# Attention and GEGLU on one core: value products ahead of the second exponential tile in all steps with a counted ScalarE backlog

## The chip, the core and the metric

The kernel runs on one core of a Trainium2 chip. The core has five engines, each with its own stream of instructions, that meet only through semaphores: TensorE (PE, matrix products; PEld are its weight loads), VectorE (DVE), ScalarE (ACT), GpSimd (POOL) and SyncE (SP, which issues the transfers). Matrix products land in PSUM, which has eight banks here of 128 x 512 float32. The metric is the device time of one execution in microseconds (us), lower is better. The kernel before took 1220.43 us, the median of three runs between 1219.77 and 1221.08.

## The reference

A transformer block on x of 2048 x 512 in bfloat16, with 32 heads of 16 columns, followed by a gated feed-forward layer of width 1792:

```
h   = x + attention(layernorm(x))           # q,k,v = x @ wqkv ; o @ wo
        scores = (q @ k^T) * 16**-0.5        # 32 heads, 2048 x 2048 each
        p = softmax(scores) ; o = p @ v
h2  = h + (gelu(n @ w_gate) * (n @ w_up)) @ w_down,   n = layernorm(h)
```

With 32 heads the scores are 32 x 2048 x 2048 numbers, and each of them passes VectorE once (for the maximum of its row) and ScalarE once (for its exponential).

## The kernel before, in words

**A program that is written by a planner.** The Python code is run once when the kernel is built. It walks through a loop of *ticks* (variable `tick`, L1645 to L1755), and in each tick it appends instructions to the lists of the five engines. A class `Plan` records for each buffer who wrote and who read it last and puts in the semaphore waits. An engine runs its own list strictly in this order. What stands behind a waiting instruction on the same engine waits as well. `group_begin` and `group_end` collect all waits of the instructions between them at the first one.

**Units.** The attention is cut into 64 units (`units`). A unit is 16 ticks long and covers four heads and 256 rows of queries (in the last units eight heads and 128 rows) against all 2048 keys. It is passed through twice. In the first pass (p1) a *score pair* of two 128 x 512 tiles is computed per tick (`p1_pair`, matmul at L886, into PSUM banks 0 to 3, two pairs of banks in turn) and VectorE takes the row maxima of both tiles in one instruction (`p1_consume`, L901). GpSimd turns the maxima of a unit into a correction of the queries (`negm_part`, `negm_pre`, `negm_post`). In the second pass (p2), 24 ticks behind the first (`P2_START`), the transposed scores are computed again, now with the maximum subtracted, in two *tiles* per tick (`p2_tile`, matmuls at L977). ScalarE takes the exponential of each (`p2_consume`, L1006) and writes it to a ring of tiles (PTM, PTE, PTG). These tiles use PSUM banks 4 to 7.

**Joint units.** In 14 units (`JOINT`) the tick with remainder 14 is dropped: its row maxima and those of the tick with remainder 10 are taken together at the latter by a fused add and maximum (L898), which uses differences of scores made ahead of time by `item_diff` (L1110, L1112) and taken out of PSUM by ScalarE (L1115). The dropped tick puts the second pass behind (`behind`), and it catches up with a third tile in some odd ticks (`more`).

**Dense items.** All other matrix work is cut into items of a few *pieces*: projections (`item_projT`, `item_projV`), value products (`item_pv`), output projection (`item_oproj`), gate, up and down (`item_gate`, `item_up`, `item_down` and their halves), differences. `dense.piece()` emits one piece and returns its cost in columns. One piece is emitted per tick, as a rule after both exponential tiles of that tick. Where no piece is at hand, `dummy` (L1621) puts in filling matmuls, whose results nobody uses.

**Value products.** `item_pv(ui)` multiplies the exponentials of a unit with the values. It has four pieces, `p` = 0 to 3, due at the ticks with remainders 7, 8, 9 and 10, each of 16 or 32 small matmuls (L1023). After the last one ScalarE copies the sum out of PSUM to `OB` (through `evac_act`, L730), and a transfer (L1051) and GpSimd (L1065, L1070) do the rest.

**PSUM banks of the second pass.** Banks 4 to 7 stand in one list, `banks.free`; `take` removes the first, `give` appends at the end. A tile takes a bank when its matmuls are emitted and gives it back when its exponential is emitted. A dense item keeps a bank from its first to its last piece. A later taker's matmul waits on the semaphore of the ScalarE instruction that read the bank last.

**The order in a tick.** The score pair and the first tile (one group of waits), the second tile, in some ticks a third one, then the row maxima, the exponentials, then the dense piece or fill:

```
            t2l = [next_tile()] if p2_ok and p1_ok else []
            P.group_end("pe")
            if p2_ok and p1_ok:
                behind[0] -= 1
                if dense.plain and tick - th_step[0] == 2 and not more:
                    mid = dense.piece()
                t2l.append(next_tile())
```

So there is an exception (L1692): two ticks after a tanh of the feed-forward part was put on ScalarE (`th_step`, set at L1297), and if the next piece is one of the middle pieces of a value product (`dense.plain`, set at L1028 to be true ahead of pieces 1 and 2, false ahead of the last), that piece is emitted ahead of the second tile.

**The count of ScalarE's backlog.** `act_lag` is the planner's estimate, in us, of the work that ScalarE has been given beyond what it can do: `act_tick` adds 0.478 for each exponential of the tick and takes off 1.135 for the tick, `act_more` adds the cost of other work. It is a number in the program and not measured.

Of the kernel before, what the change touches and what calls it, by code (L numbers as in the profile page):

```python
# [248 lines left out]
def bass_sequential_preLN__mha_block__geglu_ffn__prompt_kernel(nc, A_x, A_wqkv, A_wo, B_x, B_w_gate, B_w_up, B_w_down, out):  # L249
    dbg = None  # L250
    with ExitStack() as es:
# [81 lines left out]
        OB = at("OB", [128, 2, 256], BF16)  # L333
# [10 lines left out]
        pbank = es.enter_context(nc.psum_tensor("pbank", [128, 8, 512], FP32))  # L344
# [195 lines left out]
        class Dense:  # L540
            def __init__(self):
                self.prio = []
                self.ready = []
                self.extra = []
                self.gen = None
                self.under = None
                self.plain = False
                self.bank = None
                self.banks = [7, 3, 4, 5]
                self.rr = 0  # L550
                self.pause = 0
                self.single = False
                self.done = 0
                self.now = 0
# [152 lines left out]
        pool = PoolStream()  # L707

        act_lag = [0.0]
        th_step = [-9]  # L710
        def act_more(cost):
            act_lag[0] += cost
        def act_tick(exps):
            act_lag[0] = max(0.0, act_lag[0] + 0.478 * exps - 1.135)
        dve_free = [False]

        def evac_act(o_ap, i_ap, reads, writes, scale=None, extra=(), bias=None, then=None, cost=0.48):
# [291 lines left out]
        def item_pv(b, ui, ps=(0, 1, 2, 3)):  # L1009

            gi, slot = units[ui]
            pt_t = PV_T if ui < NU - 1 else PV_TL
            for p in ps:
                while not force[0] and dense.now < P2_START + 16 * ui + pt_t[p]:
                    yield ("wait", 1)
                for m in (2 * p, 2 * p + 1):
                    n, c0, s_ = (2, 0, slot) if ui < UB else (4, 128 * (m // 4), slot + m // 4)
                    qn = 512 // n
                    for i in range(n):
                        kt = 2 * m + i if ui < UB else 4 * (m % 4) + i  # L1020
                        for g in range(4):
                            pi = pt_of[(ui, m, g)]
                            P.op("pe", lambda e, g=g, kt=kt, pi=pi, i=i, s_=s_, c0=c0, qn=qn: e.matmul(pbank[32 * g:32 * g + 17, b, c0:c0 + qn], VA[:, kt, 4 * s_ + g, :],  # L1023
                                                                                                      PTt(pi)[:, qn * i:qn * i + qn], start=(kt == 0), stop=(kt == NT - 1), tile_position=(0, 32 * g)),
                                 reads=[("V", kt), "VA_ones", ("PT", pi)], writes=[("pb", b)], sig=(g == 3 and i == n - 1))
                    for g in range(4):
                        pt_busy.discard(pt_of.pop((ui, m, g)))
                dense.plain = p != ps[-1] and p + 1 != ps[-1]  # L1028
                if p != ps[-1]:
                    yield 2  # L1030
            if ui == NU - 1:
                col = ps[0] // 2
                evac_act(OA[:, 1, 256 * col:256 * col + 128], pbank[:, b, 128 * col:128 * col + 128], [("pb", b)], [("OA", 1, col), ("RB", 1)], cost=0.2)
                if col == 0:
                    dense.add(item_ofin, gi, front=True, est=3, not_before=dense.now + 3)
                    return 2
            else:
                evac_act(OB[:, ui % 2, :], pbank[:, b, 0:256], [("pb", b)], [("OB", ui % 2)], cost=0.27, then=lambda: o_turn(ui))
            pv_done.add(ui)
            return 2  # L1040

# [4 lines left out]
        def o_turn(ui):  # L1046
            gi, slot = units[ui]
            par = ui % 2
            assert not ob_busy.get(par), "GpSimd too far behind"
            ob_busy[par] = True  # L1050
            P.dma("sp", lambda e: e.dma_start_transpose(out=OBT[:, par, :, :], in_=OB[:, par, :]), ("obT", par), reads=[("OB", par)], writes=[("OBT", par)])  # L1051
            o4 = OBT[:, par].rearrange("p q (g i) -> p q g i", i=32)
            ks, slots = ((0, 1), (slot,)) if ui < UB else ((half(ui),), (slot, slot + 1))
            defer(5, lambda: o_norm(gi, slots, ks, par, o4, ("OBT", par), ob_busy))
# [229 lines left out]
        def gelu_chain(par, dE, w=512):  # L1284

            th_ready[par] = False
            gs, ts_ = g_sb[:, par, 0:w], th_sb[:, par, 0:w]
            o = lambda cost, fn, reads, extra=(): (cost if w == 512 else 0.6 * cost, lambda: P.op("pool", fn, reads=reads, writes=[("th", par)], extra_deps=extra))
            def later(n):
                if not force[0] and (tight() or dense.gen is not None and dense.cur is item_pv and dense.now % 16 in (9, 10)):  # L1290
                    defer(1, lambda: later(n))
                    return
                if not force[0] and (act_lag[0] + (0.48 if dense.gen is not None and dense.cur in (item_gate, item_up, item_gate_h, item_up_h) else 0) > LAG_TH + SLOPE * n or poly_end[par] > TICK * dense.now + POLY):
                    defer(1, lambda: later(n + 1))
                    return
                act_more(0.54 if w == 512 else 0.32)
                th_step[0] = dense.now  # L1297
                P.op("act", lambda e: e.activation(out=ts_, in_=ts_, func=ACT.Tanh, scale=GC), reads=[("th", par)], writes=[("th", par)])  # L1298
                defer(1, second)
            def poly_done():  # L1300
                poly_end[par] = pool.t
                defer(TANH_LAG, lambda: later(0))
            def second():
                def done():
                    th_ready[par] = True
                pool.add([o(0.62, lambda e: e.tensor_scalar(out=ts_, in0=ts_, scalar1=1.0, scalar2=0.5, op0=ALU.add, op1=ALU.mult), [("th", par)]),  # L1306
                          o(1.27, lambda e: e.tensor_tensor(out=ts_, in0=ts_, in1=gs, op=ALU.mult), [("th", par), ("g", par)])], then=done)  # L1307
            pool.add([o(1.04, lambda e: e.tensor_tensor(out=ts_, in0=gs, in1=gs, op=ALU.mult), [("g", par)], dE),  # L1308
                      o(0.62, lambda e: e.tensor_scalar(out=ts_, in0=ts_, scalar1=0.044715, scalar2=1.0, op0=ALU.mult, op1=ALU.add), [("th", par)]),
                      o(1.27, lambda e: e.tensor_tensor(out=ts_, in0=ts_, in1=gs, op=ALU.mult), [("th", par), ("g", par)])], then=poly_done)  # L1310
# [325 lines left out]
        J_ = sorted(JOINT)  # L1636
        J_PREP = {max(60, 16 * (J_[i - 1] if i else 0) + 12, 16 * J_[i] - 48 if J_[i] > 50 else 0): J_[i] for i in range(len(J_))}
        ticking[0] = True
        def next_tile():
            n = 2 * t2 - behind[0]  # L1640
            st, jj = n // 2, n % 2
            ui_ = st // 16
            t = p2_tile(ui_, st % 16, 1 - (st + P2_START) % 2, jj)
            return ui_, t
        while True:  # L1645
            p1_ok = tick < 16 * NU
# [42 lines left out]
            P.group_end("pe")  # L1689
            if p2_ok and p1_ok:  # L1690
                behind[0] -= 1
                if dense.plain and tick - th_step[0] == 2 and not more:  # L1692
                    mid = dense.piece()
                t2l.append(next_tile())
                if more:
                    behind[0] -= 1
                    t2l.append(next_tile())
                behind[0] += 1
            elif p2_ok and tick % 2 == 0:
                if tick == 16 * NU:  # L1700
                    dense.ready.sort(key=lambda it: it[0] is item_down)
                    own = dense.bank if dense.gen is not None else banks.free[0]
                    other = own ^ 1
                    banks.free = [other] if dense.gen is not None else [own, other]
                    pairs = [0, 2, 10 - (own & 6)]
                for d_ in ((0, 1) if t2 + 1 < 16 * NU else (0,)):
                    b_ = pairs.pop(0)
                    pairs.append(b_)
                    ui_, j_ = (t2 + d_) // 16, (t2 + d_) % 16
                    p2_pair(ui_, [p2_tile(ui_, j_, 1 - (tick + d_) % 2, jj, b_ + jj) for jj in (0, 1)])  # L1710
# [7 lines left out]
                    unit_end(tick // 16)  # L1718
            for ui_, t in t2l:
                p2_consume(ui_, [t])  # L1720
            if p2_ok and t2 % 16 == 0:
                if t2 // 16 < NU - 1:
                    dense.add(item_pv, t2 // 16, front=True, est=5, not_before=tick + PV_T[0])
                else:
                    for p_ in (0, 2):
                        dense.add(item_pv, NU - 1, (p_, p_ + 1), front=True, est=2, not_before=tick + PV_TL[p_])
# [71 lines left out]
```

## Time and profile before

| | |
|---|---|
| median of the runs | 1220.43 us (1219.77 to 1221.08) |
| the profiled execution | 1219.59 us, of which its span from first to last instruction is 1217.5 us |
| granted TensorE clock | 1.000 |
| row maxima L901, VectorE | 996 instructions, 1134.2 us busy, 5.7 us idle ahead of them |
| exponentials L1006, ScalarE | 2000 instructions (1357 into PTM, 407 into PTG, 236 into PTE), 1105.0 us busy, 5.1 us idle ahead of them |
| tanh L1298, ScalarE | 50 instructions, 42.9 us busy |
| copies to OB L730, ScalarE | 62 instructions, 28.3 us busy, 390 to 693 ns each |
| score pairs L886, TensorE | 2020 matmuls, 388.5 us busy |
| tiles L977, TensorE | 5120 matmuls, 513.6 us busy |
| value products L1023, TensorE | 126.0, 51.2 and 41.8 us busy by source |
| fill L1621, TensorE | 659 matmuls, 208.3 us busy |

Busy times are unions: instructions of one engine overlap in part, so a mean duration times a count is more than the busy time. The idle time of a group is that of its engine just ahead of its instructions. The profile is of one execution; its steady part, with both passes running, lies between about 45 and 1173 us from the start, and the remainder after the last row maxima is some 44 us.

### The profile page before, as it was taken

The page shows a single profiled execution, that of the slowest core. Times are in us where ns is not written, and L with a number is a line of the kernel's source. Part 1 is how long each engine was busy: PE and PEld are TensorE (multiplying, and loading weights), DVE is VectorE, ACT ScalarE, POOL GpSimd, SP SyncE. Part 2 cuts the span into 40 slices and gives each one's busy share as a digit, 9 for nine tenths or more (in the row PEclk, how much of TensorE's full clock was granted, in tenths as well). Part 3 has the DMA queues.
Part 4 walks back from the last instruction along what each step waited for, and adds up shares of the span by engine and source line. Part 5 has one row for each costly group of instructions (what it writes and reads, how often), then busy time and mean ns, then how long its engine had stood idle before and what let it go on. Part 6 is the DMA issues. An engine that isn't in the chain of part 4 may idle for free.

```text
span 1217.5 us, 35931 instructions
## 1 busy us (share of the span) xinstructions
PE 1103.6 (91%) x14692; PEld 476.7 (39%) x14838; DVE 1180.5 (97%) x1125; ACT 1188.8 (98%) x2422; POOL 837.9 (69%) x1772
## 2 busy tenths in 40 slices
PE   7899888889999989999899989999899989998998
PEld 3233332233333333334333333333334454554666
DVE  8999999999999999999999999999999999999973
ACT  7899999999999999999999999999999999999995
POOL 8567684756777586766868487684777687846772
DMA  5111104300010000110001000100001100010000
GB/s 154 28 34 27 29 24 136 93 8 11 8 28 21 12 9 10 25 23 12 10 22 17 23 8 10 25 21 15 8 8 29 26 18 16 9 27 15 18 16 19
DMA packets 69651, 32.02 MB, mean 26 GB/s; under 512 B 54768, under 2 KB 68464, under 8 KB 69488
## 3 DMA queue, kind: packets, MB, share of 16 engines
q1 hardware_dynamic: 69488, 29.71, 9.9%
q8 instruction: 118, 1.93, 0.6%
q14 instruction: 45, 0.37, 0.1%
HBM read 11.80 MB, written 2.10 MB: 11 GB/s over the span
## 4 chain that ended last, share of the span: by engine, by line
ACT 50%; DVE 40%; PE 8%; issue 2%; DMA 1%; POOL 1%
DVE PM L901 38%; ACT PTM L1006 28%; ACT PTG L1006 9%; ACT PTE L1006 5%; PE pbank L1427 2%; ACT g_sb L730 2%; ACT u_sb L730 2%; ACT th_sb L1298 1%; PE pbank L977 1%; PE pbank L1328 1%; PE pbank L886 1%; ACT OB L730 1%; DVE OA L898 1%; ACT OA L1115 1%; PE pbank L1621 1%
## 5 line engine op out<-in xcount | busy, mean ns | idle before, releaser
L901 DVE TENSOR_REDUCE PM<-pbank 128x2 f32<-128x1024 f32 x996 | 1134.2, 1215 | 5.7 <-PE pbank L977 1.8
L1006 ACT ACTIVATE PTM<-pbank 128x512 bf16<-128x512 f32 x1357 | 736.3, 737 | 3.5 <-PE pbank L977 0.6
L977 PE MATMUL pbank<-QT,KT 32*128 32x256 bf16 (+1 forms) x5120 | 513.6, 250 | 8.4 <-ACT PTG L1006 0.4
L886 PE MATMUL pbank<-KT,QT 32*128 32x512 bf16 x2020 | 388.5, 384 | 23.9 <-DVE PM L901 8.6
L1621 PE MATMUL pbank<-ones_bf,ident 128*128 128x512 bf16 x659 | 208.3, 384 | 51.8 <-ACT PTM L1006 21.7
L977 PEld LDWEIGHTS pbank<-QT,KT 32*128 32x128 bf16 x5120 | 207.6, 92 | 70.4 <-ACT PTM L1006 37.7
L886 PEld LDWEIGHTS pbank<-KT,QT 32*128 32x128 bf16 x2020 | 96.6, 91 | 341.9 <-DVE PM L901 126.7
L1006 ACT ACTIVATE PTG<-pbank 128x512 bf16<-128x512 f32 x407 | 227.0, 728 | 0.8 <-PE pbank L977 0.4
L1006 ACT ACTIVATE PTE<-pbank 128x512 bf16<-128x512 f32 x236 | 141.7, 735 | 0.8 <-PE pbank L977 0.5
L1023 PE MATMUL pbank<-PTM,VA 128*17 128x256 bf16 (+1 forms) x3470 | 126.0, 252 | 2.0 <-ACT PTM L994 0.4
L1065 POOL TENSOR_TENSOR LINV<-OBT,negone 128x8 f32<-128x8 bf16 x63 | 105.0, 1667 | 5.8 <-DMA OBT<-OB 5.6
L1621 PEld LDWEIGHTS pbank<-ones_bf,ident 128*128 128x128 bf16 x767 | 44.6, 97 | 134.1 <-ACT PTM L1006 85.3
L1308 POOL TENSOR_TENSOR th_sb<-g_sb 128x512 f32<-128x512 f32 (+1 forms) x50 | 51.1, 1022 | 63.0 <-ACT g_sb L730 63.0
L1023 PEld LDWEIGHTS pbank<-PTM,VA 128*17 128x17 bf16 x3470 | 67.0, 90 | 40.9 <-issue 21.7
L956 POOL TENSOR_TENSOR QT<-QT,STG 128x256 bf16<-128x256 bf16 x64 | 42.7, 667 | 33.9 <-DMA STG<-ST 33.4
L1307 POOL TENSOR_TENSOR th_sb<-th_sb,g_sb 128x512 f32<-128x512 f32 (+1 forms) x50 | 62.2, 1245 | 4.0
L1310 POOL TENSOR_TENSOR th_sb<-th_sb,g_sb 128x512 f32<-128x512 f32 (+1 forms) x50 | 62.3, 1246 | 1.7
L1306 POOL TENSOR_SCALAR th_sb<-th_sb 128x512 f32<-128x512 f32 (+1 forms) x50 | 30.5, 609 | 44.9 <-ACT th_sb L1298 44.8
L1427 PE MATMUL pbank<-wd_sb,GUT 128*128 128x512 bf16 x191 | 54.5, 382 | 3.4 <-ACT PTM L1006 0.8
L801 POOL TENSOR_SCALAR QT<-QKS,qmask 128x512 bf16<-128x512 bf16 x30 | 46.9, 1566 | 13.6 <-ACT QKS L730 12.8
L1383 PE MATMUL pbank<-hnT_l,wg_sb 128*128 128x256 bf16 x336 | 51.2, 275 | 3.3 <-ACT PTM L1006 0.7
L1419 POOL TENSOR_TENSOR GUT<-th_sb,u_sb 128x512 bf16<-128x512 f32 x42 | 53.3, 1268 | 1.3
(197 smaller groups left out, 1208.8 us busy)
## 6 DMA issues: line engine op xcount, KB each, us to landing
QKS<-QKS SPq DMA_DIRECT2D x27, 112.0 KB, 2.1
x_sb<-in_A_x_dram SPq DMA_DIRECT2D x4, 512.0 KB, 5.7
xres<-in_A_x_dram SPq DMA_DIRECT2D x16, 128.0 KB, 2.3
out_dram<-out_sb SPq DMA_DIRECT2D x15, 128.0 KB, 1.7
wg_sb<-in_B_w_gate_dram SPq DMA_DIRECT2D x4, 448.0 KB, 4.2
wu_sb<-in_B_w_up_dram SPq DMA_DIRECT2D x4, 448.0 KB, 4.0
wd_sb<-in_B_w_down_dram SPq DMA_DIRECT2D x3, 512.0 KB, 4.5
STG<-ST SPq DMA_TRANSPOSE x64, 2.3
```

The costliest lines, as they stand in the source:

```text
L730: P.op("act", lambda e: e.activation(out=o_ap, in_=i_ap, func=ACT.Copy, **kw), reads=reads, writes=writes, extra_deps=extra)
L886: P.op("pe", lambda e, g=g, b=b: e.matmul(pbank[:, b, :], QT[32 * g:32 * g + 32, c, slot, 128 * qt:128 * qt + 128], KT[32 * g:32 * g + 32, ...
L901: P.op("dve", lambda e: e.tensor_reduce(out=PM[:, par, qt, kc, g:g + 2], in_=pbank[:, b:b + 2, :], axis=AX.X, op=ALU.max), reads=[("pb", b ...
L977: P.op("pe", lambda e, kt=kt, i=i: e.matmul(pbank[:, b, qn * i:qn * i + qn], KT[32 * g:32 * g + 32, slot, 128 * kt:128 * kt + 128], QT[32 ...
L1006: P.op("act", lambda e, b=b, pi=pi: e.activation(out=PTt(pi), in_=pbank[:, b, :], func=ACT.Exp), reads=[("pb", b)], writes=[("PT", pi)], e ...
L1023: P.op("pe", lambda e, g=g, kt=kt, pi=pi, i=i, s_=s_, c0=c0, qn=qn: e.matmul(pbank[32 * g:32 * g + 17, b, c0:c0 + qn], VA[:, kt, 4 * s_ + ...
L1065: P.op("pool", lambda e: e.tensor_tensor(out=li, in0=o4[:, :, :, 16], in1=negone[:, 0:4 * nq].rearrange("p (q h) -> p q h", q=nq), op=ALU. ...
L1307: o(1.27, lambda e: e.tensor_tensor(out=ts_, in0=ts_, in1=gs, op=ALU.mult), [("th", par), ("g", par)])], then=done)
L1310: o(1.27, lambda e: e.tensor_tensor(out=ts_, in0=ts_, in1=gs, op=ALU.mult), [("th", par), ("g", par)])], then=poly_done)
L1419: P.op("pool", lambda e: e.tensor_tensor(out=o_ap, in0=shp(ts_), in1=shp(us), op=ALU.mult), reads=[("th", par), ("u", par)], writes=o_keys ...
L1427: P.op("pe", lambda e: e.matmul(pbank[:, b, :], GUT[:, fc, 128 * k:128 * k + 128], wd_sb[:, fc, :], start=first, stop=last), reads=[("GUT" ...
L1621: P.op("pe", lambda e: e.matmul(pbank[:, b, :], ident[:], ones_bf[:, 0:512], start=True, stop=True), reads=["ident", "ones_bf"], writes=[( ...
```

## The change

The condition for the exception is changed, and the last piece of a value product is admitted to it. Five parts:

- `th_step` goes. In its place `lag_was` keeps the count of the backlog as it stood at the last two ticks, and the piece is moved ahead of the second tile where the older of the two is at least 0.2 us (`LAG_MID`), whatever ScalarE work it came from.
- `dense.plain` is now true ahead of the last piece as well.
- The bank of the second tile is taken ahead of the piece, and handed to `next_tile` and `p2_tile`.
- While the moved piece is emitted, `dense.midway` is set. A last piece then does not emit ScalarE's copy to OB at once but puts it in `dense.held`, and it is emitted after the tick's exponentials. So ScalarE's order stays.
- The item itself ends inside the moved piece, and with it its bank is given back there, ahead of the tick's two tiles.

```
+        lag_was = [0.0, 0.0]
+        LAG_MID = 0.2
...
             act_lag[0] = max(0.0, act_lag[0] + 0.478 * exps - 1.135)
+            lag_was[:] = [lag_was[1], act_lag[0]]
...
-                dense.plain = p != ps[-1] and p + 1 != ps[-1]
+                dense.plain = p != ps[-1]
...
-                evac_act(OB[:, ui % 2, :], pbank[:, b, 0:256], [("pb", b)], [("OB", ui % 2)], cost=0.27, then=lambda: o_turn(ui))
+                def out():
+                    evac_act(OB[:, ui % 2, :], pbank[:, b, 0:256], [("pb", b)], [("OB", ui % 2)], cost=0.27, then=lambda: o_turn(ui))
+                    pv_done.add(ui)
+                if dense.midway:
+                    dense.held.append(out)
+                    return 2
+                out()
             pv_done.add(ui)
             return 2
...
-                th_step[0] = dense.now
...
-        def next_tile():
+        def next_tile(bank=None):
             n = 2 * t2 - behind[0]
             st, jj = n // 2, n % 2
             ui_ = st // 16
-            t = p2_tile(ui_, st % 16, 1 - (st + P2_START) % 2, jj)
+            t = p2_tile(ui_, st % 16, 1 - (st + P2_START) % 2, jj, bank)
...
                 behind[0] -= 1
-                if dense.plain and tick - th_step[0] == 2 and not more:
+                b_ = banks.take()
+                if dense.plain and lag_was[0] >= LAG_MID and not more:
+                    dense.midway = True
                     mid = dense.piece()
-                t2l.append(next_tile())
+                    dense.midway = False
+                t2l.append(next_tile(b_))
...
             for ui_, t in t2l:
                 p2_consume(ui_, [t])
+            while dense.held:
+                dense.held.pop(0)()
```

## The prediction, as it was put on record

> **What bounds the kernel now.** I read the page's busy times first, then its chain of waits, then the timeline of single ticks (a tick is one pass of the main loop: one score pair for VectorE, two exponential tiles for ScalarE, one dense piece).
>
> ```profile
> PE 1103.6 (91%) x14692; PEld 476.7 (39%) x14838; DVE 1180.5 (97%) x1125; ACT 1188.8 (98%) x2422; POOL 837.9 (69%) x1772
> ...
> ACT 50%; DVE 40%; PE 8%; issue 2%; DMA 1%; POOL 1%
> ...
> L901 DVE TENSOR_REDUCE PM<-pbank 128x2 f32<-128x1024 f32 x996 | 1134.2, 1215 | 5.7 <-PE pbank L977 1.8
> ```
>
> VectorE and ScalarE are both nearly full, and the chain changes between them. VectorE has the firmer limit: 996 maximum reductions (L901) with 5.7 us of idle time in all. Where nothing is late they follow each other at 1.13 us:
>
> ```profile
> 640.68 5.74 DVE L901 TENSOR_REDUCE PM<-pbank 128x2 f32<-128x1024 f32 x5
> ```
>
> Five in 5.74 us: the last takes 1.21, so four spacings of 1.13. ScalarE has room: an exponential tile takes it 0.48 us (starts below), two a tick 0.96. A tick in which VectorE starts late is lost for good; a tick in which ScalarE is late is not, unless TensorE passes the delay on. So I follow TensorE's score pair (L886), which feeds VectorE. The weight loads of TensorE in ticks 554 to 556, a step that the change touches:
>
> ```profile
> 641.11 0.09 PEld L886 LDWEIGHTS pbank<-KT,QT 32*128 32x128 bf16 x2
> 641.11 0.11 PEld L977 LDWEIGHTS pbank<-QT,KT 32*128 32x128 bf16 x2
> 641.60 0.11 PEld L977 LDWEIGHTS pbank<-QT,KT 32*128 32x128 bf16 x2 [0.37 <-ACT PTM L1006]
> 641.91 0.11 PEld L1023 LDWEIGHTS pbank<-PTG,VA 128*17 128x17 bf16 x8 [0.21 <-issue]
> ...
> 642.46 0.09 PEld L886 LDWEIGHTS pbank<-KT,QT 32*128 32x128 bf16 x2 [0.22 <-issue]
> 642.47 0.22 PEld L977 LDWEIGHTS pbank<-QT,KT 32*128 32x128 bf16 x4
> 643.07 0.11 PEld L1621 LDWEIGHTS pbank<-ones_bf,ident 128*128 128x128 bf16 x2 [0.38 <-ACT PTM L1006]
> 643.60 0.09 PEld L886 LDWEIGHTS pbank<-KT,QT 32*128 32x128 bf16 x2 [0.42 <-issue]
> ```
>
> Tick 554: score pair at 641.11, first tile at once, second tile at 641.60 after a wait for its bank, last value piece (L1023) at 641.91. Tick 555: pair at 642.46, both tiles at once (x4), fill (L1621) at 643.07. Tick 556: pair at 643.60. ScalarE meanwhile:
>
> ```profile
> 641.29 0.74 ACT L1006 ACTIVATE PTM<-pbank 128x512 bf16<-128x512 f32 x1
> ...
> 642.26 0.75 ACT L1006 ACTIVATE PTM<-pbank 128x512 bf16<-128x512 f32 x1
> 642.74 0.55 ACT L730 ACTIVATE OB<-pbank 128x256 bf16<-128x256 f32 x1
> ```
>
> The row at 642.26 is tick 554's second exponential, ending 643.01; the evacuation of the finished unit (OB) ends at 643.29.
>
> **What the change does.** The order of the two built programs agrees on ScalarE, VectorE, GpSimd and SyncE, instruction for instruction; so no DMA and no queue of SP or POOL moves, and nothing is added or removed. Only TensorE's order and the numbers of the PSUM banks differ. Value pieces ahead of the second tile rise from 27 to 67: 40 more, of which 24 are last pieces of a unit (tick mod 16 = 10) and 16 are middle or start-up pieces.
>
> **Price of moving a piece.** Tick 553 already does it:
>
> ```profile
> 640.00 0.11 PEld L977 LDWEIGHTS pbank<-QT,KT 32*128 32x128 bf16 x2
> 640.32 0.09 PEld L1023 LDWEIGHTS pbank<-PTM,VA 128*17 128x17 bf16 x1 [0.21 <-issue]
> ...
> 640.86 0.11 PEld L977 LDWEIGHTS pbank<-QT,KT 32*128 32x128 bf16 x2 [0.22 <-issue]
> ```
>
> First tile to piece 0.32, piece to second tile 0.54; that tile's exponential starts at 641.29, 0.43 after its load, and ends at 642.03. ScalarE's ends stay 0.49 apart there, since the later exponential is also shorter (0.74 against 0.82); the shortest L1006 rows are 0.59 and one after an idle start is 0.62. In tick 554 the piece would start at 641.43, the second tile at 641.97, its exponential at 642.40, ending 643.02 instead of 643.01. The move costs ScalarE 0.01 us, hidden behind the exponentials queued before it. The next pair gains: it no longer stands behind a piece that stands behind a wait.
>
> **Price of the last piece.** Finishing a unit hands its PSUM bank back. Before, this came after both tiles of the tick had handed back theirs, so the bank was last in line. Now it comes first: the free list is (one bank, the unit's bank, the two tiles' banks), and the second tile of the next tick gets the unit's bank. The waits that the program writes say so at all 24 places: tick 555's second tile waited for the exponential ending at 642.52; now it waits for the evacuation ending at 643.29, two ScalarE instructions later. Behind it on TensorE stand the dense piece or fill, then tick 556's score pair, and for that VectorE waits. Step by step, after a wait 0.05 (643.01 to 643.07 above), tile to next work 0.32, fill to pair 0.53:
>
> 643.29 + 0.01 + 0.05 = 643.35 second tile (was 642.58); 643.67 fill; 644.20 pair, was 643.60, so 0.60 late. What a pair needs to reach VectorE when late is 0.43:
>
> ```profile
> 320.29 0.09 PEld L886 LDWEIGHTS pbank<-KT,QT 32*128 32x128 bf16 x2 [0.23 <-issue]
> ...
> 320.72 2.35 DVE L901 TENSOR_REDUCE PM<-pbank 128x2 f32<-128x1024 f32 x2 [0.23 <-PE pbank L977]
> ```
>
> Tick 556's reduction started 644.07, now 644.63: 0.56 lost, the slack of 0.04 used up. The same arithmetic with each place's own rows, gains in the tick before already taken off: 6 places with difference matmuls (0.86 us from piece to pair) 3.61; 8 with fill 4.49; 6 with gate or up 3.23; the halves 1.06 (one of them, tick 954, after the piece moved in 953 gave back 0.38); one down 0.59, one projection 0.68. Together 13.7 us, on average 0.57.
>
> **Gains elsewhere.** Of the 16 other moves, six stand in joint units one tick ahead of the pair of the fused maximum, which comes 0.15 late in six of them (1.36 from the reduction before against 1.22): 0.9. Tick 889 gets 0.1 and 937 0.05; the rest sit where VectorE is not late: nothing, covered by the 0.04 to 0.2 us that their pairs have in hand, and up to the same 0.57 a place if that cover were gone, which I leave out since no bank order changes there.
>
> Sum: 13.7 - 0.9 - 0.15 = **+12.6 us**. VectorE's last reduction ends at about 1174; the rest (ScalarE 21.6 us busy of the next 22) has an unchanged order and moves along. The profiled execution took 1219.59 us for a span of 1217.5, close to the median of 1220.43; on the median this gives 1233.0.
>
> Bounds: the evacuation may take 0.55 from its later start instead of ending 0.28 after the exponential, +0.14 a place, +3.4. Downwards, VectorE's spacings after tick 192 lie 8.6 us above 1.13 in all (the fused maximum aside), of which 1.9 are under the late ticks priced above and 1.6 are credited; a ScalarE that is less behind could give the other 5 back. So 1228 to 1236.4.
>
> **Rivals.** (1) *The later wait is hidden*, faster: only the gains count, 1.1 us in the ticks behind last pieces, 1.05 above and 0.4 at tick 954, to 1217.9. It decides if tick 556's pair leaves by 643.64, which needs the evacuation over by 642.73, before the exponential ahead of it ends; against it stands the order on ScalarE. 4%. (2) *ScalarE loses too*: the evacuation at full length, 0.71 a place: 1236.4. For it: that length in the rows here. 15%. (3) *ScalarE recovers*: a later VectorE leaves it time, and the other late ticks vanish: 1228. 12%. (4) *No net effect*, the slack larger than the rows show: 1220.4, 3%. (5) *The clock drops*: TensorE would idle some 0.9 us (642.4 to 643.35 in the place above) at 24 places more. The start of this trace shows a slow stretch:
>
> ```profile
> 4.70 0.15 PEld L456 LDWEIGHTS pbank<-ones_bf,ident 128*128 128x128 bf16 x1 [0.28 <-issue]
> 5.03 3.55 PEld L456 LDWEIGHTS pbank<-ones_bf,ident 128*128 128x128 bf16 x17 [0.18 <-issue]
> ...
> PEld pbank L886 <- DVE PM L901: 126.7, 277, 1.0
> ```
>
> Loads 0.43 apart until 5.03, 0.21 after, a stretch of 3.3 us. Three ticks at half pace, each with 0.98 us of TensorE work (pair to second tile 0.12, tile to piece 0.31, piece to pair 0.55), would lose 3 x 0.83 = 2.5 a place, +60, 1293. Against it: L886 already waits up to 1.0 us (last row: total, times, longest), with a granted clock of 1.00 from 45 to 1173. 2%. The Trainium skill, "TensorE: Matmul & The Clock Gate", section "A second HAM failure mode: psum-queue depth-cycling", says that frequent short idling while PSUM banks cycle can make the clock gate oscillate; the trace of before gives no sign of it.
>
> **How the numbers follow.** My forecast has 64%. The range 1227 to 1237 takes in rivals 2 and 3 and a little more. Faster by over 0.2%, about what a measurement here can tell: rival 1, 0.04. Within: 0.03. Slower: the rest, 0.93.
>
> **What would show it.** Right: in ticks with remainder 11 behind a moved last piece, the second tile's load (L977) alone, some 0.77 us later, ended by the OB evacuation; VectorE's spacing 1.6 to 2.3 us in the tick after, in most of 24 places; L901's idle time several times 5.7 us. Wrong: second tiles still ended by exponentials, or pairs on time behind them. The fused maximum's spacing at 1.22 everywhere shows the gains.

## The result, and the profile after

The changed kernel took 1230.64 us (median of 6 runs, 1230.27 to 1232.25) against 1220.37 us for the kernel before on the same chip (6 runs, 1219.63 to 1221.08): a ratio of 1.0086, 95% interval 1.0073 to 1.0099, or +10.3 us. The profiled execution took 1230.44 us with a span of 1228.4 us, 10.9 us more than the span before; the granted clock stayed at 1.00. (In the changed kernel the lines behind the edit are numbered 4 to 9 higher: row maxima L905, tiles L981, fill L1630, score pairs L890, exponentials L1010, copies to OB L734, value products L1027.)

From the page after, the chain of waits by engine and the two groups of instructions that changed most (busy us, mean ns of one, idle us of the engine ahead of them):

```profile
ACT 55%; DVE 30%; PE 11%; issue 2%; POOL 1%; DMA 1%; POOLq 0%
...
L905 DVE TENSOR_REDUCE PM<-pbank 128x2 f32<-128x1024 f32 x996 | 1133.8, 1215 | 17.8 <-PE pbank L981 15.0
...
L981 PE MATMUL pbank<-QT,KT 32*128 32x256 bf16 (+1 forms) x5120 | 508.1, 250 | 22.6 <-ACT OB L734 18.2
```

VectorE's work is the same (1134 us); its idle time ahead of the maxima rose from 5.7 to 17.8 us, by 12.1, and 15.0 of it is put down to a score tile. (The maxima read the score pair, L890; the profile names the tile L981 whose loads start with the pair's, 645.16 and 645.17 below.) TensorE in turn waits for the OB copy ahead of the tiles, a releaser that this group did not have before. From the view of all waits (total, times, longest):

```profile
PEld pbank L981 <- ACT OB L734: 26.0, 24, 1.1
```

24 times: the number of places that were counted from the written waits. At the place that the prediction worked through (ticks 554 to 556), TensorE's weight loads after the change:

```profile
645.16 0.10 PEld L890 LDWEIGHTS pbank<-KT,QT 32*128 32x128 bf16 x2
645.17 0.11 PEld L981 LDWEIGHTS pbank<-QT,KT 32*128 32x128 bf16 x2
645.49 0.11 PEld L1027 LDWEIGHTS pbank<-PTG,VA 128*17 128x17 bf16 x8 [0.21 <-issue]
...
646.03 0.11 PEld L981 LDWEIGHTS pbank<-QT,KT 32*128 32x128 bf16 x2 [0.22 <-issue]
...
647.40 0.11 PEld L981 LDWEIGHTS pbank<-QT,KT 32*128 32x128 bf16 x2 [1.14 <-ACT OB L734]
647.72 0.11 PEld L1630 LDWEIGHTS pbank<-ones_bf,ident 128*128 128x128 bf16 x2 [0.21 <-issue]
648.26 0.09 PEld L890 LDWEIGHTS pbank<-KT,QT 32*128 32x128 bf16 x2 [0.42 <-DVE PM L905]
```

ScalarE's copy and VectorE's maxima there:

```profile
646.96 0.39 ACT L734 ACTIVATE OB<-pbank 128x256 bf16<-128x256 f32 x1
```

```profile
644.74 3.47 DVE L905 TENSOR_REDUCE PM<-pbank 128x2 f32<-128x1024 f32 x3
648.69 2.36 DVE L905 TENSOR_REDUCE PM<-pbank 128x2 f32<-128x1024 f32 x2 [0.48 <-PE pbank L981]
```

The moved piece (645.49) stands ahead of tick 554's second tile (646.03), as the change says. Tick 555's second tile then waits until the copy ends (646.96 + 0.39 = 647.35) and leaves at 647.40; fill 0.32 later, pair 0.54 after that, reduction 0.43 after that. The three maxima ahead of it end at 648.21, so VectorE stands idle for 0.48 us; by the starts of single reductions the spacing is 1.69 us, 0.56 over the usual 1.13.

### The profile page after: what moved, and what is told of

Read it like the earlier page. It is cut to its first block, busy times and chain, and to the rows that moved or that the text cites. A ratio compares the mean times of both kernels' runs of the same rounds, so it can differ in the third digit from the quotient of the medians.

```text
span 1228.4 us, 36067 instructions
## 1 busy us (share of the span) xinstructions
PE 1130.0 (92%) x14838; PEld 475.8 (39%) x14838; DVE 1179.6 (96%) x1125; ACT 1194.6 (97%) x2422; POOL 837.5 (68%) x1772
## 3 DMA queue, kind: packets, MB, share of 16 engines
q8 instruction: 118, 1.93, 0.7%
## 4 chain that ended last, share of the span: by engine, by line
ACT 55%; DVE 30%; PE 11%; issue 2%; POOL 1%; DMA 1%; POOLq 0%
ACT PTM L1010 31%; DVE PM L905 28%; ACT PTG L1010 10%; ACT PTE L1010 6%; PE pbank L1436 3%; PE pbank L981 2%; ACT g_sb L734 2%; ACT u_sb L734 2%; ACT th_sb L1307 2%; PE pbank L890 2%; PE pbank L1337 1%; ACT OB L734 1%; PE pbank L1630 1%; PE pbank L1027 1%; DVE OA L902 1%
## 5 line engine op out<-in xcount | busy, mean ns | idle before, releaser
L905 DVE TENSOR_REDUCE PM<-pbank 128x2 f32<-128x1024 f32 x996 | 1133.8, 1215 | 17.8 <-PE pbank L981 15.0
L1010 ACT ACTIVATE PTM<-pbank 128x512 bf16<-128x512 f32 x1357 | 732.5, 711 | 7.6 <-PE pbank L981 4.2
L981 PE MATMUL pbank<-QT,KT 32*128 32x256 bf16 (+1 forms) x5120 | 508.1, 250 | 22.6 <-ACT OB L734 18.2
L890 PE MATMUL pbank<-KT,QT 32*128 32x512 bf16 x2020 | 393.4, 384 | 26.3 <-DVE PM L905 10.0
L1630 PE MATMUL pbank<-ones_bf,ident 128*128 128x512 bf16 x767 | 234.7, 385 | 28.0 <-ACT PTM L1010 4.7
L981 PEld LDWEIGHTS pbank<-QT,KT 32*128 32x128 bf16 x5120 | 205.4, 92 | 91.2 <-ACT PTM L1010 30.0
L890 PEld LDWEIGHTS pbank<-KT,QT 32*128 32x128 bf16 x2020 | 99.8, 91 | 342.7 <-DVE PM L905 141.1
L1010 ACT ACTIVATE PTG<-pbank 128x512 bf16<-128x512 f32 x407 | 224.4, 695 | 1.6 <-PE pbank L981 1.1
L1010 ACT ACTIVATE PTE<-pbank 128x512 bf16<-128x512 f32 x236 | 138.4, 708 | 0.8 <-PE pbank L981 0.5
L1027 PE MATMUL pbank<-PTM,VA 128*17 128x256 bf16 (+1 forms) x3470 | 126.1, 252 | 1.9 <-ACT PTM L998 0.4
L1630 PEld LDWEIGHTS pbank<-ones_bf,ident 128*128 128x128 bf16 x767 | 44.7, 97 | 129.2 <-ACT PTM L1010 81.8
L1027 PEld LDWEIGHTS pbank<-PTM,VA 128*17 128x17 bf16 x3470 | 67.1, 90 | 40.7 <-issue 22.0
L960 POOL TENSOR_TENSOR QT<-QT,STG 128x256 bf16<-128x256 bf16 x64 | 42.7, 667 | 38.8 <-DMA STG<-ST 38.6
L1436 PE MATMUL pbank<-wd_sb,GUT 128*128 128x512 bf16 x210 | 57.9, 383 | 0.6
```

The source lines that it names most:

```text
L890: P.op("pe", lambda e, g=g, b=b: e.matmul(pbank[:, b, :], QT[32 * g:32 * g + 32, c, slot, 128 * qt:128 * qt + 128], KT[32 * g:32 * g + 32, ...
L905: P.op("dve", lambda e: e.tensor_reduce(out=PM[:, par, qt, kc, g:g + 2], in_=pbank[:, b:b + 2, :], axis=AX.X, op=ALU.max), reads=[("pb", b ...
L981: P.op("pe", lambda e, kt=kt, i=i: e.matmul(pbank[:, b, qn * i:qn * i + qn], KT[32 * g:32 * g + 32, slot, 128 * kt:128 * kt + 128], QT[32 ...
L1010: P.op("act", lambda e, b=b, pi=pi: e.activation(out=PTt(pi), in_=pbank[:, b, :], func=ACT.Exp), reads=[("pb", b)], writes=[("PT", pi)], e ...
L1436: P.op("pe", lambda e: e.matmul(pbank[:, b, :], GUT[:, fc, 128 * k:128 * k + 128], wd_sb[:, fc, :], start=first, stop=last), reads=[("GUT" ...
L1630: P.op("pe", lambda e: e.matmul(pbank[:, b, :], ident[:], ones_bf[:, 0:512], start=True, stop=True), reads=["ident", "ones_bf"], writes=[( ...
```

## The experiments

Ten kernels ran. The theory: the loss lies in the hand-back of the unit's PSUM bank, which after the change comes ahead of the tick's own tiles, and not in the move of the piece. The rivals: the move itself costs, or ScalarE's order does. "Shift" below is how much later the last row maximum starts than in the kernel before, by the two profiled executions; a tick's share is the change of that shift over the tick. A part of the shift stands already ahead of the first maximum (0.5 us in e1, 0.9 in e10, 0.3 in e3, e5 and e9, 0.2 in e7, under 0.1 in the others).

| kernel | us, median | ratio to before, 95% | shift, us |
|---|---|---|---|
| the change | 1230.64 | 1.0086 (1.0073 to 1.0099) | +10.9 |
| e1_bank_last | 1220.47 | 1.0001 (0.9993 to 1.0010) | +0.5 |
| e2_middle_only | 1220.12 | 0.9999 (0.9990 to 1.0008) | +0.7 |
| e3_bank_alone | 1229.90 | 1.0079 (1.0065 to 1.0093) | +11.1 |
| e4_copy_between | 1220.83 | 1.0005 (0.9996 to 1.0014) | +1.3 |
| e5_bank_first | 1239.37 | 1.0158 (1.0142 to 1.0174) | +19.0 |
| e6_bank_third | 1224.84 | 1.0035 (1.0021 to 1.0049) | +4.3 |
| e7_all_moves | 1225.58 | 1.0042 (1.0029 to 1.0055) | +4.8 |
| e8_no_fill | 1257.71 | 1.0300 (1.0286 to 1.0315) | +38.6 |
| e9_before_short_copy | 1217.10 | 0.9972 (0.9961 to 0.9983) | -2.9 |
| e10_last_short_copy | 1217.04 | 0.9972 (0.9962 to 0.9983) | -2.0 |

**The moves without the early bank (e1).** In the changed kernel, the bank of a moved last piece is handed back at the end of the list, behind those of the tick's tiles:

```
                         if self.single:
-                            banks.give(ended)
+                            if self.midway:
+                                self.late.append(ended)
+                            else:
+                                banks.give(ended)
...
             while dense.held:
                 dense.held.pop(0)()
+            while dense.late:
+                banks.free.insert(9, dense.late.pop(0))
```

> All 40 moves of the change stay; only the bank that a moved last piece frees is handed back after the tick's two tiles have handed back theirs, as in the kernel before. Theory (the second tile's wait for the OB copy costs the time): the 24 losses vanish and the gains stay, the second tile of the next tick waits for an exponential again; 2.0 to 3.0 us under the kernel before, 1217.4 to 1218.4. Rival A (the place of the last piece ahead of the tile costs the time): 1229 to 1231 as with the change. Rival B (the moved middle pieces cost part of it): between, over 1221.

```profile
L909 DVE TENSOR_REDUCE PM<-pbank 128x2 f32<-128x1024 f32 x996 | 1134.3, 1224 | 6.9 <-PE pbank L985 2.6
```

From the page of e1, the row maxima: with all 40 moves in place and only the bank last, the idle time is back to 6.9 us and the whole loss is gone. So the moves do not cost it. But the time is that of the kernel before, and not 2 to 3 us less: the expected gain is missing.

**Only the middle pieces (e2).** In the changed kernel, last pieces are not admitted: `dense.plain = p != ps[-1] and p + 1 != ps[-1]`.

> The new backlog condition, but last pieces are not admitted: 16 pieces move, 24 do not, no bank order changes. Theory: only the gains of the middle pieces, 1.0 to 1.7 us under the kernel before, 1218.7 to 1219.4. Rival A (last pieces' place): the same. Rival B (middle pieces cost): over 1221.

No change either, where 1.0 to 1.7 us less were expected: these moves gain nothing that lasts.

**Only the bank (e3).** In the kernel before, with no instruction moved on any engine, the unit's bank goes into the list where the change puts it:

```
                         if self.single:
-                            banks.give(ended)
+                            if self.second:
+                                banks.free.insert(1, ended)
+                            else:
+                                banks.give(ended)
```

(`second` is set for a last piece in the ticks in which the change would move it.)

> The kernel before with every instruction where it stood; only at the 24 places the bank that the last value piece frees is put second in the list instead of last, so that the next tick's second tile waits for the OB copy. Theory: the whole loss without any move, 24 x 0.5 to 0.57 = 12 to 13.7 us, 1232 to 1234, more than the change because its gains are missing. Rival A and B (the moves cost it): 1220.4, no change.

The maxima of e3 on its page, and the wait in the view of all waits:

```profile
L910 DVE TENSOR_REDUCE PM<-pbank 128x2 f32<-128x1024 f32 x996 | 1135.4, 1223 | 16.3 <-PE pbank L986 13.0
```

```profile
PEld pbank L986 <- ACT OB L739: 17.6, 24, 1.0
```

The same 24 waits and +9.5 us, with every instruction in the order of the kernel before. The intervals of e3 and of the change overlap: the hand-back alone accounts for the result. The 1229.9 us lie below the 1232 to 1234 that were expected; the places give 11.3 us (table in the next section) instead of 12 to 13.7, and some of the gains that were thought to be missing are there without a move (same section).

**The copy earlier (e4).** The change with its banks, but the OB copy is put between the tick's two exponentials:

```
-            for ui_, t in t2l:
+            for n_, (ui_, t) in enumerate(t2l):
+                if n_ == 1:
+                    while dense.held:
+                        dense.held.pop(0)()
                 p2_consume(ui_, [t])
```

> The change with its bank order, but ScalarE copies to OB between the tick's two exponentials instead of after both. Theory (it is the time at which that copy ends that counts): the copy ends some 0.6 us earlier, which is just what the score pair of the tick after next lacks, so the loss of 0.57 a place shrinks to 0 to 0.1; 1217.5 to 1220.5. Rival A (place of the last piece): 1229 to 1231. A rival in between, that the copy then waits for the piece's end and holds up ScalarE: 1222 to 1226.

The second tile still waits for the copy at 23 of the 24 places, but the copy now ends one exponential sooner, and the places with fill lose 0.11 us on average (0.07 to 0.08 at four of eight) instead of 0.60 in the change. The time is just above the range that was expected, since the gains are missing here as in e1. So a wait on the copy is harmless where the copy comes in time; it is its place on ScalarE that makes the bank late.

**Other places in the list (e5, e6).** The kernel of e1 with `insert(0, ...)` and `insert(2, ...)`:

> The change, but the bank of a moved last piece goes to the head of the list, so that the next tick's score pair itself (with the first tile) waits for the OB copy. Theory (what counts is which instruction of the next tick waits for that copy): the pair is 0.8 us late at once and the next one cannot make it up; 24 x 0.8 = 19, some 1238 to 1241. Rival (the moved piece's place costs it): 1230 as with the change.

> The change, but that bank goes third in the list, so that in the next tick the dense piece or fill waits for the OB copy and both tiles do not. Theory: the pair after it is late by 0.2 to 0.25 us at each of the 24 places, half of the change's loss, with all places together 5 us, 1224 to 1227. Rival: 1230.

First in the list it is taken by the first tile of the next tick, whose waits are collected at the score pair; third, by the dense piece or fill. Idle time ahead of the maxima was 25.8 and 11.4 us. First, second, third and last give +19.0, +10.9, +4.3 and +0.5 us of shift: the price falls with each place that the bank moves back.

**Every value piece moved (e7).** The kernel of e1 with `LAG_MID = 0.0`: 186 pieces stand ahead of the second tile, 119 more than in e1.

> The bank at the end of the list as in the kernel before, and the threshold of the backlog at 0, so that 186 pieces move instead of 67. Theory (the gains of moved pieces are given back some ticks later, where TensorE waits for ScalarE, which is full there): no change, 1219.8 to 1221.2. Rival C (each move gains or costs for good): moves of 0.14 us a place would show as 1203 or 1237; already a lasting 0.02 a place would be 3 us.

A miss: +4.3 us against e1 by traces, 5.1 by medians. VectorE's share of it is spread over several remainders; ScalarE's tells where it comes from. Compared with e1, the end of ScalarE's work of a tick moves back by 8.3 us in sum in the ticks with remainders 8, 9 and 10, where the pieces are, 0.07 for each of the 119, and forward again by 3.5 us in ticks with remainders 4 to 6 and 12 to 15. Busy times between 400 and 800 us, of the kernel before and of e7:

```profile
core 0: us, PE busy (x) PEld busy (x) DVE busy (x) ACT busy (x) POOL busy (x), PEclk, DMA share, GB/s
...
400.00:800.00 400.00, 366.78 (x4223) 141.36 (x4265) 398.71 (x366) 398.63 (x824) 280.98 (x592) 1.00 0.07 16
```

```profile
400.00:800.00 400.00, 367.38 (x4204) 142.23 (x4247) 396.84 (x364) 398.53 (x818) 278.79 (x587) 1.00 0.08 16
```

The third and fourth pairs of numbers are VectorE and ScalarE. In the kernel before both are busy for all but 1.3 and 1.4 us of 400; in e7 VectorE loses 1.9 us, while ScalarE is as busy as before but gets through 818 instructions instead of 824. A busy share does not show that: an exponential that follows at once overlaps the one before (starts 0.48 apart, 0.6 to 0.9 long), and one whose scores come a little late loses overlap, not busy time. The whole span of e7 says so:

```profile
PE 1115.1 (91%) x14692; PEld 482.3 (39%) x14838; DVE 1181.6 (97%) x1125; ACT 1193.0 (98%) x2422; POOL 837.4 (69%) x1772
```

The same 2422 instructions keep ScalarE busy for 4.2 us more than in the kernel before (1188.8), which is most of what the time grew by, while its idle time ahead of the exponentials hardly changes (5.5 against 5.1 us).

**Without fill (e8).** To see if the fill behind a late exponential is what takes the gains back, fill is left out in the ticks with a counted backlog:

```
-            if (cost or 0) < want:
+            if (cost or 0) < want and not (p1_ok and p2_ok and lag_was[1] >= LAG_MID):
```

> The 67 moves with the bank at the end of the list, and no fill in ticks in which the counted backlog of ScalarE is 0.2 us or more (576 of 767 fill matmuls are left out). In the trace the fill of such a tick waits for an exponential and the next score pair stands behind it, 0.53 us. If that fill is what gives the gains back, the six gains of 0.14 stay and late ticks behind a fill vanish: 2 to 6 us under the kernel before, 1214 to 1218.5. If ScalarE itself is the limit there (the tiles behind the pair wait for it anyway): 1219.5 to 1220.5. If TensorE's clock drops without the fill: over 1225.

The third case came true. From the stretches of e8, the granted clock is the third number from the end:

```profile
300.00:600.00 300.00, 260.68 (x2908) 102.78 (x2923) 288.52 (x266) 289.62 (x593) 199.80 (x440) 0.89 0.07 16
600.00:900.00 300.00, 263.27 (x2898) 102.67 (x2916) 288.14 (x264) 288.54 (x591) 201.34 (x441) 0.88 0.07 16
...
1210.00:1256.00 46.00, 39.93 (x787) 28.43 (x793) 19.16 (x40) 33.75 (x48) 16.34 (x26) 1.00 0.07 20
```

The score pairs on its page, against a mean of 384 ns in e1:

```profile
L894 PE MATMUL pbank<-KT,QT 32*128 32x512 bf16 x2020 | 431.1, 421 | 110.7 <-DVE PM L909 62.7
```

So the run says nothing on its question; what it says of the clock stands in the last section.

**ScalarE relieved (e9, e10).** The OB copy takes 64 of 256 columns, in the kernel before (e9) and in that of e1 (e10); both leave out a part of the attention's output. The order of the work does not change.

```
-evac_act(OB[:, ui % 2, :], pbank[:, b, 0:256], ...
+evac_act(OB[:, ui % 2, 0:64], pbank[:, b, 0:64], ...
```

> The kernel before, with ScalarE's copy of a finished unit taking 64 of its 256 columns (the other columns keep the ones put there at the start, so part of the attention's output is left out). No other instruction and no order changes. It takes some 0.16 us a copy from ScalarE (0.23 us lie between an exponential over 512 columns and a copy over 256), 62 copies, 9.9 us in all. Theory: ScalarE is as full as VectorE between 45 and 1173 us, and a late pair can come from it everywhere, so relief of ScalarE shows in the time: 1215 to 1219 us against 1220.4. Rival (the prediction's reading, ScalarE has room, VectorE alone is the limit): 1220 to 1221 us, no change.

> All 40 moves with the bank handed back at the end of the list, and the same short copy. Compare with the kernel before with the short copy. Theory: what the moves gain for VectorE was taken back six ticks later by ScalarE's own work; with ScalarE relieved by 0.16 us ahead of that tick the losses of 0.13 us in the ticks with remainder 0 behind joint units (288, 416, 544, 672, 800, 976) are gone. Either the gain of 0.14 us at each joint unit then stays, and this kernel is 0.6 to 2 us faster than the other with the short copy, or the relief alone has made these pairs punctual in both, and the two are equal with no loss of 0.13 us in either. Rival (TensorE's order, the fill behind a late exponential, takes the gains back whatever ScalarE does): the losses of 0.13 us at these ticks remain.

Both took 3.3 us less than the kernel before, though only ScalarE was relieved, by 0.16 us in each of 62 copies. A rival is that the shorter copy frees its bank sooner. The instructions that wait for the copy, and the pair behind them, stand in ticks with remainders 11 and 12, and in e9 these hold 0.4 of the 3.2 us that are gained between the first and the last maximum, so it can explain a small part only. e9 and e10 took the same time: with ScalarE relieved the moves gain nothing; at the joint units the pairs are punctual without them. VectorE's rows around tick 288, the timeline of the kernel before, of e1 and of e10:

```profile
337.93 10.57 DVE L901 TENSOR_REDUCE PM<-pbank 128x2 f32<-128x1024 f32 x9
```

```profile
338.44 10.69 DVE L909 TENSOR_REDUCE PM<-pbank 128x2 f32<-128x1024 f32 x9
```

```profile
338.40 10.45 DVE L910 TENSOR_REDUCE PM<-pbank 128x2 f32<-128x1024 f32 x9
```

Nine maxima behind a joint unit take 0.12 us longer in e1 than before, and 0.12 less in e10. By single ticks, the change of the shift against the kernel before:

| | tick 282 (fused maximum) | tick 288 |
|---|---|---|
| the change | -0.14 | -0.07 |
| e1, moves only | -0.14 | +0.13 |
| e3, bank only | -0.14 | -0.03 |
| e9, short copy only | -0.14 | -0.09 |
| e10, moves and short copy | -0.14 | -0.10 |

The gain at the joint unit comes with the move alone, with a later VectorE alone, and with a relieved ScalarE alone. Where ScalarE is as late as before (e1), it is given back six ticks on. There the two engines meet: in all eleven other kernels the shift of VectorE at tick 288 is that of the end of ScalarE's work in that tick, to 0.04 us, though at tick 282 they lay up to 0.2 us apart either way. Over the steady part of e1 only tick 777 (-0.21 us, behind the transfer named at the end) changes the end of ScalarE's work by more than 0.1 us against the kernel before: to ScalarE the moves make no difference.

## Why the prediction held, point by point

**The bank: right.** Which instruction waits, for what and how often came out as worked: 24 waits of the second tile on the copy, and at the place shown 0.05, 0.32, 0.54 and 0.43 us for the steps behind it. e1 and e3 show it from both sides: without the bank nothing is lost, and with the bank alone nearly all is.

**The sum over the places: one term off.** Each place's loss, by the work that stands behind the second tile. What the tick just before had gained is taken off, and at one of the halves, as in the prediction, also the 0.34 us that the piece moved in tick 953 had gained (predicted 0.38; no move and no such gain in e3):

| behind the second tile | places | predicted us | the change, us | e3, us |
|---|---|---|---|---|
| fill | 8 | 4.49 | 4.81 | 4.50 |
| gate or up | 6 | 3.23 | 3.29 | 3.15 |
| difference matmuls | 6 | 3.61 | 1.80 | 1.75 |
| halves, down, projection | 4 | 2.33 | 2.33 | 1.93 |
| sum | 24 | 13.7 | 12.2 | 11.3 |

The failing step is "6 places with difference matmuls (0.86 us from piece to pair) 3.61". Such a place after the change, tick 523, TensorE's weight loads:

```profile
611.43 0.09 PEld L981 LDWEIGHTS pbank<-QT,KT 32*128 32x128 bf16 x1 [1.14 <-ACT OB L734]
611.44 0.09 PEld L1120 LDWEIGHTS pbank<-KT,QT 32*128 32x128 bf16 x1
...
611.97 0.10 PEld L1630 LDWEIGHTS pbank<-ones_bf,ident 128*128 128x128 bf16 x1 [0.42 <-issue]
612.29 0.10 PEld L890 LDWEIGHTS pbank<-KT,QT 32*128 32x128 bf16 x2 [0.23 <-DVE PM L905]
```

The loads of the difference matmuls (L1120, L1122) go in between those of the tile, 0.01 us behind it, and the pair follows the tile by 0.86 us; it is so at all six places. The 0.86 from piece to pair was right. Ahead of it I had put the usual 0.32 us from tile to next work, a step that is 0.01 us here: six times 0.3, the 1.8 us by which this term is too large. The rows have the same shape for both (weights of 32x128), as for a pair and its first tile, which also start 0.01 us apart (645.16 and 645.17 above); the 0.32 was read from pieces and fill, whose weights have 128 rows. It also shows that "strictly in this order" is too strong for TensorE: loads of the work behind the tile start ahead of the tile's second load.

**"Gains elsewhere": near the right size, the wrong reason.** All other ticks of the change sum to -1.4 us, predicted -1.05. That they come so near is luck in part: ticks 360 and 776 (last section) add +0.7 us, which is put down to a transfer there. The fused maxima are in the sum with six times 0.14; their spacing fell from 1.27 to 1.13, the same step as the 1.36 and 1.22 of the prediction, which are both 0.09 too large. But e3 has five of these six without any move, since a later VectorE lets ScalarE catch up, and in e1 and e2, where the moves stand alone, nothing remains. The step took a pair that comes sooner for time gained. It is gained only where ScalarE has time as well.

**"ScalarE has room": wrong.** It rested on 0.96 us of exponentials in a tick of 1.13, without the copies, tanh and evacuations, and the shares (97% and 98%) were not read by stages: most of ScalarE's gaps lie at the start and the end. Between 400 and 800 us both engines are equally full, and e9 shows the price: 3.3 us less for relieving ScalarE. Rival 3 (ScalarE recovers) is thus true in part, for the fused maxima and a few small ticks.

**"The move costs ScalarE 0.01 us": right where the planner counts a backlog, wrong elsewhere.** e1 shows it right for the 40 moves; e7's further 119 cost ScalarE 0.07 us each. So, as far as e7 shows, it is the backlog condition that makes the moves of the change harmless.

**Rival 2** (the copy at full length from its later start) fell: the late copy is shorter, 0.38 to 0.49 us at the 24 places, against 0.39 to 0.69 before (0.39 and 0.55 at the place shown). **Rival 5** (the clock) fell: 1.00, with TensorE waiting up to 0.9 us at 24 places more. It was not far off, as e5 shows in the last section. **Rivals 1 and 4** needed pairs on time behind the wait, and they were late.

Together: the places gave 1.4 us less than forecast, the other ticks 0.3 less; against the spans that is 10.9 instead of 12.6, against the medians 10.3. No version that ran beats the kernel before by what can be measured: e2, the best that computes the reference, is at 0.9999 (0.9990 to 1.0008).

## What to carry to other kernels

When an instruction that ends a work item moves forward, look at what the program gives back at that moment: here a list of banks took a new order, and the next taker inherited a reader that stands two instructions further back on another engine. Hand a buffer back in the order in which its last reader will be done. And before a gain on one engine is counted, look at the other engine in the same stretch, not over the whole span; where both are full, a gain on one is on loan until the other has time.

## What was not expected of the hardware

**Fill holds the clock.** e8 leaves out 576 of the 767 fill matmuls and nothing else. In the stretch from 300 to 600 us TensorE was busy for 283.35 us in e10 (whose trace has all 767 fill records, unlike that of e1 with 659) and for 260.68 in e8, at slower matmuls, and the granted clock went from 1.00 to between 0.88 and 0.91 in all four stretches between 45 and 1210 us, back to 1.00 behind them: 1257.71 us against 1220.47 in e1, +37 us. So the clock of these kernels hangs on the fill. The Trainium skill, "TensorE: Matmul & The Clock Gate", section "A second HAM failure mode: psum-queue depth-cycling", tells of frequent short idling between groups of matmuls that makes the clock swing. e8 agrees: the mean of 0.902 is made of 39 stretches at 0.50, of 3.4 to 10.2 us and 246 us in all, with 1.00 between them, though the longest idle time of TensorE between 45 and 1170 us is 1.0 us. The change, with 24 new waits against 294 ticks without fill in e8, does not show it.

In between lies e5, where the score pair itself waits for the copy (up to 1.3 us, against 1.1 for the tile in the change). It has two stretches of 3.4 us at 0.50, at two of its 24 places; the first one:

```profile
761.30:764.71 3.41, 3.36 (x22) 0.70 (x23) 3.02 (x3) 3.08 (x7) 2.45 (x5) 0.50 0.10 19
```

The maxima in and right behind each stretch (ticks 653 and 654, 781 and 782) are late by another 0.7 us. So what rival 5 describes does occur in this kernel, at waits a little longer than those of the change. Where the limit lies was not measured.

**A transfer that varies.** At ticks 360 and 776 a unit's first tile waits for GpSimd's correction of the queries, and that for a transposed transfer (STG). It landed 3.2 us after its issue in the execution before and 3.6 in the one after at tick 360 (3.5 and 3.8 at tick 776, 2.4 in e1). These two ticks gave +0.40 and +0.32 us in the change and +0.04 and -0.44 in e1, with the same transfers in the same order: so shifts that differ by half a microsecond between two profiled executions are not read as an effect.
